# A quarter of the first batch's up layer as seven block products, with the set-up of the weights reordered around it

## The chip, the cores and the metric

One core of one Trainium2 chip. The time is the device time of one execution in microseconds; the numbers compared are medians over runs, and the traces are one profiled execution each. Engines: TensorE (PE in the profile, its weight loads PEld), VectorE (DVE), ScalarE (ACT), GpSimd (POOL), SyncE (SP).

## The reference

Linear attention with projected keys and values, and then a feed-forward layer with a maximum of two linear maps:

```
k_proj = E @ k,  v_proj = F @ v                       # per batch and head: 64 x 64
attn   = softmax(q @ k_proj.T / 8) @ v_proj
x      = attn, heads side by side                     # 8192 tokens x 512
out    = maximum(x @ w1, x @ w2) @ w_out              # w1, w2: 512 x 1024, w_out: 1024 x 512
```

Batch 8, 8 heads, sequence 1024, head size 64. Inputs and output are float32; the kernel works in float16 with float32 sums.

## The kernel before

**What is computed.** maximum(a, b) = relu(a - b) + b, so with wd = w1 - w2 and m = w2 @ w_out the output is relu(x @ wd) @ w_out + x @ m. relu(x @ wd) is the "up" layer, the rest the "down" layer. Each batch is cut into two units of 512 tokens; U[b, o] is unit o of batch b.

**Seven products.** From unit U[1, 0] on the up layer, for all units the down layer, and once the product m = w2 @ w_out, go by seven block products in place of eight (Strassen's scheme in Winograd's form). The factors are cut into 2 x 2 blocks; VectorE makes four sums or differences of each factor: of x (sums_x into s_x), of the up layer's result g (sums_g into s_g), of w2 transposed (sums_m), of w_out and m (step_t into T_sb), of wd (step_tw into t_w). The products run in the order 1, 2, 6, 5, 7, 3, 4. Products 1, 6, 7 and 4 add up in one PSUM bank (X) which ScalarE copies out after 1, 6 and 7 (keep) because the running sums are needed; 2 has a bank (Y); 5 and 3 share that bank again (Z). The blocks of the result are additions of these on VectorE.

**Batch 0.** Its up layer is done directly, in pieces: up_slots(t, j) gives eight pieces u_j[0] to u_j[7] for unit j (u0 and u1), each of four matmuls of 128 x 512 (line 525) into one bank, emptied by a relu on ScalarE (line 534; for piece 3 on VectorE, line 536). Meanwhile the weights arrive and are prepared: step_wd and step_wd_rows (wd[1], wd[2], wd[3] are the second, third and fourth quarter of the columns of wd = w1 - w2, on VectorE, line 549), and step_w2t (w2 transposed by TensorE in four groups of eight 128 x 128 blocks, line 557, each copied out by ScalarE, line 563). The list `slots` gives the order in which all this is issued. m_steps, at its end, is the product m by seven products of eight matmuls of 256 columns (line 634).

**What sets the order.** The schedule is written by hand: the program order of `slots`, with further steps hung behind a slot by at_slot, is the order of every engine's queue; each engine takes its queue strictly in order, and semaphores make it wait for data and for buffers. After batch 0's pieces come the slots ("P", n, p, i), the down products of unit n in pieces (line 838), with the attention of the next batches and their up products (up_steps, line 746) laid between them.

**Buffers.** PSUM has four banks mm0 to mm3 and two double banks "att". mm_bank() without a number takes the four in turn, mm_bank(n=...) a given one. In SBUF `box` names the large buffers big0 to big3 that held E and F, w1, w2 and the transposed w2 and are used again for the sums once those are read. `soft` has five tiles for exponentials and sums of the attention; `ppool` holds the copies that keep makes.

Of the kernel before, what the change touches and what calls it, by code (L numbers as in the profile page):

```python
# [9 lines left out]
FP32 = mybir.dt.float32  # L10
# [9 lines left out]
def kernel(  # L20
# [495 lines left out]
    def up_slots(t, j):  # L516
        t["gt", j] = gt = gpool.tile([128, NFB, HALF], FP16, tag="gt", name="gt_sb")
        for fb in range(NFB):
            def up(fb=fb, r0=0, r1=NDC):
                if r0 == 0:  # L520
                    t["up", j, fb] = mm_bank(n=None if r1 == NDC else first_banks[j][fb])
                h_ps = t["up", j, fb]
                order = range(NDC) if fb < 2 else (0, 2, 1, 3)
                for r in order[r0:r1]:
                    nc.tensor.matmul(  # L525
                        out=h_ps,
                        lhsT=wd_sb[:, r, fb * 128 : (fb + 1) * 128],
                        rhs=t["xt"][:, r, :, j * W : (j + 1) * W],
                        start=(r == 0), stop=(r == NDC - 1),
                    )  # L530
                if r1 < NDC:
                    return
                if fb != 3:
                    nc.scalar.activation(out=gt[:, fb, :], in_=h_ps, func=ACTF.Relu)
                else:
                    nc.vector.tensor_scalar_max(gt[:, fb, :], h_ps, 0.0)
            yield up
# [78 lines left out]
    def m_steps():  # L616
        st = {}
        two = lambda ap: ap.rearrange("q (i m) -> q i m", i=2)

        def product(k, name, n):  # L620
            if n is not None:
                st[name] = mm_bank(n=n)
            bank = st[name]
            Bb = lambda h, c: wo_sb[:, h * NG : (h + 1) * NG, c * CH : (c + 1) * CH]
            T = lambda i: T_sb[:, i, 0:NG, :]
            a, w_ = {
                1: lambda: (m_blk(0, 0), Bb(0, 0)), 2: lambda: (m_blk(0, 1), Bb(1, 0)),
                3: lambda: (m_sums[3], Bb(1, 1)), 4: lambda: (m_blk(1, 1), T(3)),
                5: lambda: (m_sums[0], T(0)), 6: lambda: (m_sums[1], T(1)),
                7: lambda: (m_sums[2], T(2)),  # L630
            }[k]()
            for i in range(2):
                for c in range(NG):
                    nc.tensor.matmul(  # L634
                        out=bank[:, i * CH : (i + 1) * CH],
                        lhsT=a[:, c, i * 128 : (i + 1) * 128],
                        rhs=w_[:, c, :],
                        start=(n is not None and i == 0 and c == 0),
                        stop=(c == NG - 1), skip_group_check=True,
                    )  # L640
            return bank

        def block(j, c):
            return m_sb[:, 2 * j : 2 * j + 2, c * CH : (c + 1) * CH]

        def add(j, c, x, y):
            nc.vector.tensor_tensor(out=block(j, c), in0=two(x), in1=two(y), op=ALU.add)
# [23 lines left out]
        return [p1, p2, p6, p5, p7, p3, p4]  # L671

    def s_g(i):
        return box[2].rearrange("q (s n m) -> q s n m", s=4, n=NG)[:, i]

    def s_x(i, u):
        n = u["n"] % 3
        half = box[1 if n < 2 else 3].rearrange("q (h s n m) -> q h s n m", h=2, s=4, n=NX)
        return half[:, n % 2, i]

    def t_w(i):
        return box[0].rearrange("q (s n m) -> q s n m", s=4, n=NX)[:, i]

    def step_tw(i):
        sub4(
            [t_w(i) for i in range(4)],
            lambda h, c: wd_sb[:, h * NX : (h + 1) * NX, c * HALF : (c + 1) * HALF], (i,),
        )

    def x_blk(u, j, h):  # L690
# [25 lines left out]
        step_s(u, g_blk, s_g, which)  # L716

    def keep(tag, bank, copy=nc.scalar.copy):
        x = ppool.tile([128, 512], FP32, tag=tag, bufs={"pu": 3, "pd": 4}[tag], name="p_sb")
        copy(out=x, in_=bank)  # L720
        return x

    def new_gt(u):
        u["gt"] = gpool.tile([128, NFB, HALF], FP16, tag="gt", name="gt_sb")


    def up_steps(u):
        for d in range(2):
            st = {}
            xbank, ybank = (2, 3) if d == 0 else (3, 2)  # L730

            def product(k, name, n, st=st, d=d):
                if n is not None:
# [21 lines left out]
            two = lambda ap: ap.rearrange("q (m n) -> q m n", m=2)  # L755

            def c_blk(j, c, d=d):
                return u["gt"][:, c * NG + 2 * d : c * NG + 2 * d + 2, j * W : (j + 1) * W]
# [4 lines left out]
            def relu(ap):  # L763
                nc.vector.tensor_scalar_max(ap, ap, 0.0)  # L764

            def p1(st=st, product=product, xbank=xbank, d=d):
                if d == 0:
                    new_gt(u)
                st["s1"] = keep("pu", product(1, "X", xbank))

            def p2(st=st, product=product, ybank=ybank, add=add, c_blk=c_blk):
                add(0, 0, product(2, "Y", ybank), st["s1"])
                relu(c_blk(0, 0))

            def p6(st=st, product=product):
                st["u1"] = keep("pu", product(6, "X", None))

            def p5(st=st, product=product, ybank=ybank):
                st["s5"] = keep("pu", product(5, "Z", ybank))

            def p7(st=st, product=product):
                st["u2"] = keep("pu", product(7, "X", None))
# [230 lines left out]
    def loads(b, *names):  # L1013
        for n in names:
# [12 lines left out]
            elif b_ < B:  # L1027
                load_all(tiles[b_], b_, n, {"k": k, "v": v, "q": q}[n])

    slots = [  # L1030
        (0, lambda: u0[0](r0=2)), (1, lambda: u0[1](r0=2)), (None, lambda: loads(1, "v", "q", "k")),
        (None, lambda: step_w2t(256, True)),
        (2, lambda: u1[0](r0=2)), (3, lambda: u1[1](r0=2)),
        (None, wd[1]), (4, u0[2]), (5, u0[3]),
        (None, wd[2]), (6, u1[2]), (7, u1[3]), (None, wt[2]), (None, wt[3]), (8, u0[4]), (9, u0[5]), (None, wd[3]),
        (10, u1[4]), (11, u1[5]), (12, u0[6]), (13, u0[7]),
        (14, u1[6]), (15, u1[7]),
        *((16 + n, x) for n, x in enumerate(m_steps())),
    ]
    slots = [((0, n), x) for n, x in slots]  # L1040

# [27 lines left out]
        steps.setdefault(key, []).append(lambda: s(*a))  # L1069


    for key, s_, *a in (
        *((10 + i // 2, sums_m, i) for i in range(4)), *((12 + i, step_t, 0, (i,)) for i in range(4)),
        (11, open_box, 1), (11, sums_x, U[0, 0], (0, 1)),
        (15, open_box, 0, 2), (17, sums_x, U[0, 0], (2, 3)),
        (18, sums_g, U[0, 0], (0, 1)), (19, sums_g, U[0, 0], (2, 3)), (22, open_box, 3),
    ):
        at_slot((0, key), s_, *a)


    t = tiles[1]
    at_slot((0, 22), new_attn, t)
    at_slot((0, 22), lambda: turn.__setitem__(slice(None), [2, 3]))
    for n, x in enumerate((
        "", "", "", "", "", "kv", "", "kpt", "qt00 qt10", "", "sc00 sc10", "qt01",
        "qt11 dn00 in00 dn10 in10", "", "", "at00 AT10 sc01",
    )):
        key = ("P", n // 15, (n - 1) // 2 % 7, (n - 1) % 2) if n else (0, 22)
        for name in x.split():
            if name[0] == "k":  # L1090
                if name == "kpt":
# [12 lines left out]
        if n in (2, 3):  # L1104
            for i in range(2):
                at_slot(key, step_tw, 2 * (n - 2) + i)
        if 6 <= n < 10:
            at_slot(key, sums_x, U[0, 1], ((2, 0, 1, 3)[n - 6],))


    t = tiles[2]
# [252 lines left out]
```

## Time and profile before

| | |
|---|---|
| median of 3 runs | 319.89 us (319.88 to 319.95) |
| the profiled execution, its own time | 320.29 us |
| its span, first to last instruction | 318.5 us |
| granted TensorE clock, mean | 1.000 |
| TensorE busy | 311.8 us (98%) |
| VectorE, ScalarE, GpSimd busy | 241.1, 206.0, 41.4 us |
| matmuls of the direct up pieces (line 525) | 64, from 23.8 us on |
| first matmul of m (line 634), first of the down products (line 838) | 39.4 us, 45.5 us |

Timeline rows show the start, the length, the engine, the line, the operation with its tiles, the shapes and the count of instructions merged into one row; an idle time of the engine just ahead of it stands in brackets with what ended it. A matmul's row ends when its last result is out, so rows of TensorE overlap and its pace is read from starts.

### The profile page before, as it was taken

The numbers are of one execution on the slowest core, as the hardware profiler recorded it, in microseconds if no ns is written. First come the engines' busy times: TensorE is split into PE (matmuls) and PEld (weight loads), VectorE is DVE, ScalarE is ACT, GpSimd is POOL, SyncE is SP. The second block draws the span as 40 slices with busy tenths as digits, with TensorE's granted clock in tenths as the row PEclk, the third lists the DMA queues.
The fourth block names the chain that finished last, engine by engine and source line by source line (L and its number), as shares of the span: only waits on it lengthen the run. The fifth ranks groups of instructions, "written<-read, shape, count | busy, mean of one in ns | idle before, by whom it ended". The sixth has DMA issues, their size and how long they took to land.

```text
span 318.5 us, 9309 instructions
## 1 busy us (share of the span) xinstructions
PE 311.8 (98%) x3922; PEld 253.8 (80%) x3922; DVE 241.1 (76%) x442; ACT 206.0 (65%) x373; POOL 41.4 (13%) x63
## 2 busy tenths in 40 slices
PE   7999999999999999999999999999999999999996
PEld 3565588888887888788887888788887888888885
DVE  2366889887969696896969696996969696969883
ACT  2386742777776777477776777477776777765541
POOL 8259102004000300012000400030000000000000
PEclk9999999999999999999999999999999999999999
DMA  7999999999989999799999999989979131313124
GB/s 179 206 202 197 207 207 201 207 156 141 204 163 183 171 209 245 208 188 147 225 229 219 169 199 245 221 155 174 230 153 217 42 101 36 102 35 102 36 99 136
DMA packets 76684, 53.71 MB, mean 169 GB/s; under 512 B 29664, under 2 KB 76128, under 8 KB 76640
## 3 DMA queue, kind: packets, MB, share of 16 engines
q0 software_dynamic: 30688, 28.05, 56.0%
q1 hardware_dynamic: 45664, 24.85, 33.1%
q8 instruction: 31, 0.51, 0.6%
q10 hardware_dynamic: 288, 0.20, 0.2%
q14 instruction: 13, 0.11, 0.1%
HBM read 57.15 MB, written 16.78 MB: 232 GB/s over the span
## 4 chain that ended last, share of the span: by engine, by line
PE 95%; DMA 3%; ACT 1%; DVE 1%; issue 0%; POOLq 0%
PE mm_ps L838 47%; PE mm_ps L746 27%; PE mm_ps L525 4%; PE mm_ps L195 4%; PE att_ps L352 4%; PE mm_ps L340 2%; DMA k_sb<-in_k_dram 2%; PE mm_ps L634 2%; PE att_ps L237 1%; PE mm_ps L311 1%; PE mm_ps L153 1%; DMA out_dram<-o_sb 1%; PE att_ps L340 0%; DVE qt_sb L316 0%; ACT ld_sb L388 0%
## 5 line engine op out<-in xcount | busy, mean ns | idle before, releaser
L720 ACT COPY p_sb<-mm_ps 128x512 f32<-128x512 f32 x179 | 101.7, 592 | 49.2 <-PE mm_ps L746 27.3
L838 PEld LDWEIGHTS <-big 128*128 128x128 f16 x768 | 73.5, 98 | 11.8 <-issue 3.6
L838 PE MATMUL mm_ps<-T_sb,big 128*128 128x256 f16 x576 | 76.9, 273 | 0.0
L761 DVE TENSOR_TENSOR gt_sb<-mm_ps,p_sb 128x512 f16<-128x512 f32 x56 | 38.5, 688 | 43.0 <-PE mm_ps L746 41.6
L746 PE MATMUL mm_ps<-big,big 128*128 128x256 f16 x336 | 50.4, 273 | 0.0
L746 PEld LDWEIGHTS <-big 128*128 128x128 f16 x448 | 43.8, 98 | 5.1
L838 PE MATMUL mm_ps<-wo_sb,gt_sb 128*128 128x256 f16 x256 | 42.6, 273 | 0.0
L838 PEld LDWEIGHTS <-gt_sb 128*128 128x128 f16 x376 | 35.7, 98 | 6.7 <-issue 2.7
L469 ACT ACTIVATE ex_sb<-mm_ps 128x512 f16<-128x512 f32 x50 | 27.2, 597 | 18.0 <-PE mm_ps L340 12.3
L746 PEld LDWEIGHTS <-wd_sb 128*128 128x128 f16 x336 | 32.9, 98 | 3.8
L746 PE MATMUL mm_ps<-xt_sb,wd_sb 128*128 128x256 f16 x224 | 32.8, 273 | 0.0
L499 DVE TENSOR_TENSOR xt_sb<-att_ps,ld_sb 128x1024 f16<-128x1024 f32 x26 | 31.7, 1219 | 0.2
L303 POOL COPY junk<-qt_sb 1x1 f16<-1x1 f16 x6 | 2.6, 432 | 172.3 <-DMA qt_sb<-q_sb 172.3
L838 PE MATMUL mm_ps<-m_sb,xt_sb 128*128 128x256 f16 x128 | 24.4, 273 | 0.0
L869 DVE TENSOR_TENSOR o_sb<-mm_ps,p_sb 128x512 f32<-128x512 f32 x32 | 21.9, 683 | 2.8 <-ACT p_sb L898 2.0
L764 DVE TENSOR_SCALAR gt_sb<-gt_sb 128x512 f16<-128x512 f16 (+1 forms) x60 | 20.9, 348 | 2.1
L706 DVE TENSOR_TENSOR big<-gt_sb 128x1024 f16<-128x1024 f16 x32 | 21.9, 683 | 0.0
L838 PE MATMUL mm_ps<-wo_sb,big 128*128 128x256 f16 x128 | 21.5, 273 | 0.0
L807 ACT ACTIVATE gt_sb<-mm_ps 128x512 f16<-128x512 f32 x28 | 16.8, 601 | 5.7 <-PE mm_ps L746 5.7
L838 PE MATMUL mm_ps<-T_sb,gt_sb 128*128 128x256 f16 x120 | 20.3, 273 | 0.0
L838 PEld LDWEIGHTS <-xt_sb 128*128 128x128 f16 x188 | 18.3, 98 | 2.3 <-issue 0.2
L761 DVE TENSOR_TENSOR gt_sb<-p_sb 128x512 f16<-128x512 f32 x28 | 19.1, 682 | 0.6 <-ACT p_sb L720 0.6
(121 smaller groups left out, 434.8 us busy)
## 6 DMA issues: line engine op xcount, KB each, us to landing
out_dram<-o_sb SPq DMA_DIRECT2D x62, 256.0 KB
k_sb<-in_k_dram POOLq DMA_DIRECT2D x7, 1024.0 KB, 9.7
v_sb<-in_v_dram POOLq DMA_DIRECT2D x7, 1024.0 KB, 15.4
q_sb<-in_q_dram POOLq DMA_DIRECT2D x5, 1024.0 KB, 22.8
q_sb<-in_q_dram POOLq DMA_DIRECT2D x6, 512.0 KB, 15.9
big<-in_moe_w_dram POOLq DMA_DIRECT2D x12, 128.0 KB, 6.4
v_sb<-in_v_dram POOLq DMA_DIRECT2D x4, 256.0 KB, 14.0
wo_sb<-in_moe_w_out_dram POOLq DMA_DIRECT2D x1, 1024.0 KB, 10.4
```

Source lines behind the costliest of these rows:

```text
L195: nc.tensor.matmul(out=kv_ps[r * KP : (r + 1) * KP, h * D : (h + nh) * D], lhsT=eft[i][:, c, :], rhs=t[w][:, h0 + h : h0 + h + nh, c, :], ...
L352: nc.tensor.matmul(out=dst(r ^ (hh % 2))[hh * Z : (hh + 1) * Z, :], lhsT=weights(rows, hh), rhs=ex[rows, hh % 2, hh // 2 * W : (hh // 2 + ...
L469: nc.scalar.activation(out=t["ex", g, j][:, e, :], in_=banks[e], func=ACTF.Exp, scale=scale)
L499: nc.vector.tensor_tensor(out=x_out(t, g, j).rearrange("q z o n -> q o z n"), in0=at_ps.rearrange("q o (z n) -> q o z n", z=2), in1=ld[:, ...
L706: nc.vector.tensor_tensor(out=S(i), in0=S(0) if x is None else x, in1=y(), op=op)
L720: copy(out=x, in_=bank)
L746: nc.tensor.matmul(out=bank[:, m * W : (m + 1) * W], lhsT=w_[:, n_, (2 * d + m) * 128 : (2 * d + m + 1) * 128], rhs=a[:, n_, :], start=(n ...
L761: nc.vector.tensor_tensor(out=c_blk(j, c), in0=two(x), in1=two(y), op=ALU.add)
L764: nc.vector.tensor_scalar_max(ap, ap, 0.0)
L807: nc.scalar.activation(out=out, in_=in_, func=ACTF.Relu)
L838: nc.tensor.matmul(out=bank[i][:, 0:CH] if two_banks else bank[:, i * CH : (i + 1) * CH], lhsT=a(c)[:, i * 128 : (i + 1) * 128], rhs=w_(c) ...
L869: nc.vector.tensor_tensor(out=o_sb, in0=two(x), in1=two(y), op=ALU.add)
```

## The change

- Four of the sixteen pieces of batch 0's up layer, u1[2], u1[3], u1[6] and u1[7], that is half of the columns' pairs of unit U[0, 1], are computed by seven block products, up_steps(U[0, 1], (1,)), called S1, S2, S6, S5, S7, S3, S4 below. They use banks 2 and 3, and keep their copies in `soft` tiles.
- The remaining direct pieces after the first four use bank fb % 2 (0 or 1), where they took the four banks in turn.
- The last two transposed groups of w2 go to the attention banks. The first chain of m's products (M1, M6, M7, M4) also uses an attention bank, M2 bank 0 and M5 and M3 bank 1, so m's products use three tiles.
- The first addition of the quarter (c0, after S2) is put behind the third weight difference, and its last two additions with their relu (rest) go into the down products. The first addition of m's product (M_add) goes behind two sums of g.
- The differences of wd, t_w, are made in two halves of their columns: step_tw(i, 1) ahead of S6, step_tw(i, 0) in the down products, where the x sums of U[0, 1] were; those now come first, ahead of u0[2].
- The x sums of units with n % 3 below 2 and the g sums go to the parts of w1's and w2's buffers that are read out, without opening these buffers anew.
- What was hung behind slots by at_slot in this section is written into `slots` itself.

```diff
-                    t["up", j, fb] = mm_bank(n=None if r1 == NDC else first_banks[j][fb])
+                    t["up", j, fb] = mm_bank(n=first_banks[j][fb] if r1 < NDC else fb % 2)
...
-                st[name] = mm_bank(n=n)
+                st[name] = att_banks()[:, 0, :] if n == 3 else mm_bank(n=n)
...
-            st["s1"] = keep("pu", product(1, "X", 2))
+            st["s1"] = keep("pu", product(1, "X", 3))
...
-            add(0, 0, product(2, "Y", 3), st["s1"])
+            st["c0"] = product(2, "Y", 0)
...
-    def step_tw(i):
+    def step_tw(i, d):
+        f0 = d * CH
         sub4(
-            [t_w(i) for i in range(4)],
-            lambda h, c: wd_sb[:, h * NX : (h + 1) * NX, c * HALF : (c + 1) * HALF], (i,),
+            [t_w(i)[:, :, f0 : f0 + CH] for i in range(4)],
+            lambda h, c: wd_sb[:, h * NX : (h + 1) * NX, c * HALF + f0 : c * HALF + f0 + CH], (i,),
         )
...
-    def up_steps(u):
-        for d in range(2):
+    def up_steps(u, halves=range(2)):
+        for d in halves:
             st = {}
-            xbank, ybank = (2, 3) if d == 0 else (3, 2)
+            tag = "soft" if u["b"] == 0 else "pu"
+            xbank, ybank = (2, 3) if d == 0 or u["b"] == 0 else (3, 2)
...
+                bank = product(2, "Y", ybank)
+
+                def c0():
+                    add(0, 0, bank, st["s1"])
+                    relu(c_blk(0, 0))
+
+                if u["b"] == 0:
+                    u["c0"] = c0
+                else:
+                    c0()
...
+                if u["b"] == 0:
+                    def rest(u=u, st=st, d=d, bank=bank):
+                        add(0, 1, bank, st["u1"])
+                        add(1, 1, st["u2"], st["s5"])
+                        relu(up_gt(u)[:, NG + 2 * d : NG + 2 * d + 2, :])
+
+                    u["rest"] = rest
+                    return
...
-        (0, lambda: u0[0](r0=2)), (1, lambda: u0[1](r0=2)), (None, lambda: loads(1, "v", "q", "k")),
-        (None, lambda: step_w2t(256, True)),
-        (2, lambda: u1[0](r0=2)), (3, lambda: u1[1](r0=2)),
-        (None, wd[1]), (4, u0[2]), (5, u0[3]),
-        (None, wd[2]), (6, u1[2]), (7, u1[3]), (None, wt[2]), (None, wt[3]), (8, u0[4]), (9, u0[5]), (None, wd[3]),
-        (10, u1[4]), (11, u1[5]), (12, u0[6]), (13, u0[7]),
-        (14, u1[6]), (15, u1[7]),
-        *((16 + n, x) for n, x in enumerate(m_steps())),
+        lambda: u0[0](r0=2), lambda: u0[1](r0=2), lambda: loads(1, "v", "q", "k"),
+        lambda: step_w2t(256, True),
+        lambda: u1[0](r0=2), lambda: u1[1](r0=2), wd[1], lambda: sums_x(U[0, 1], range(4)),
+        u0[2], u0[3], S1, S2, lambda: step_w2t(512, True), lambda: step_w2t(768, True), wd[2],
+        lambda: U[0, 1]["c0"](), u0[4], u0[5], wd[3], lambda: [step_tw(i, 1) for i in range(4)] and None,
+        u1[4], S6, u1[5], S5, u0[6], S7, u0[7],
+        lambda: [sums_m(i) for i in range(4)] and None, S3, S4,
+        lambda: step_t(0, (0, 1)), M1, lambda: step_t(0, (2, 3)), M2, lambda: sums_x(U[0, 0], (0, 1)),
+        M6, lambda: sums_g(U[0, 0], (0, 1)), M_add, M5, lambda: sums_g(U[0, 0], (2, 3)), M7, M3, M4,
...
+        if n == 2:
+            at_slot(key, sums_x, U[0, 0], (2, 3))
+        if n == 3:
+            at_slot(key, lambda: U[0, 1]["rest"]())
         if 6 <= n < 10:
-            at_slot(key, sums_x, U[0, 1], ((2, 0, 1, 3)[n - 6],))
+            at_slot(key, step_tw, n - 6, 0)
```

More of the change, by code (lines that the diff above doesn't have):

```diff
@@ L1028, in loads @@
                 load_all(tiles[b_], b_, n, {"k": k, "v": v, "q": q}[n])
+    open_box(0)
+    S1, S2, S6, S5, S7, S3, S4 = up_steps(U[0, 1], (1,))
+    M1, M2, M6, M5, M7, M3, M4, M_add = m_steps()
     slots = [
-        (0, lambda: u0[0](r0=2)), (1, lambda: u0[1](r0=2)), (None, lambda: loads(1, "v", "q", "k")),
-        (None, lambda: step_w2t(256, True)),
-        (2, lambda: u1[0](r0=2)), (3, lambda: u1[1](r0=2)),
-        (None, wd[1]), (4, u0[2]), (5, u0[3]),
-        (None, wd[2]), (6, u1[2]), (7, u1[3]), (None, wt[2]), (None, wt[3]), (8, u0[4]), (9, u0[5]), (None, wd[3]),
-        (10, u1[4]), (11, u1[5]), (12, u0[6]), (13, u0[7]),
-        (14, u1[6]), (15, u1[7]),
-        *((16 + n, x) for n, x in enumerate(m_steps())),
+        lambda: u0[0](r0=2), lambda: u0[1](r0=2), lambda: loads(1, "v", "q", "k"),
[7 more added lines that the diff above has]
+        M6, lambda: sums_g(U[0, 0], (0, 1)), M_add, M5, lambda: sums_g(U[0, 0], (2, 3)), M7, M3, M4,
+        lambda: (open_box(3), new_attn(tiles[1]), turn.__setitem__(slice(None), [2, 3])) and None,
     ]
-    slots = [((0, n), x) for n, x in slots]
+    slots = [(("M", n), x) for n, x in enumerate(slots)]
     kv_units = range(3, 2 * B - 4, 2)
@@ L1069, in at_slot @@
         steps.setdefault(key, []).append(lambda: s(*a))
[L1072 to L1078, printed above, removed]
     t = tiles[1]
-    at_slot((0, 22), new_attn, t)
-    at_slot((0, 22), lambda: turn.__setitem__(slice(None), [2, 3]))
     for n, x in enumerate((
```

42 lines of the change are left out of this document (22 added, 20 removed).

## The prediction

> **What bounds the kernel now.** I read the page first (busy shares, then the chain that ended last), then TensorE's own waits, then the timeline of each engine from 27 to 60 us, where the change lies.
>
> ```profile
> span 318.5 us, 9309 instructions
> PE 311.8 (98%) x3922; PEld 253.8 (80%) x3922; DVE 241.1 (76%) x442; ACT 206.0 (65%) x373; POOL 41.4 (13%) x63
> PE 95%; DMA 3%; ACT 1%; DVE 1%; issue 0%; POOLq 0%
> PE att_ps L352 <- ACT vp_sb L207: 0.5, 1, 0.5
> PE att_ps L352 <- ACT ex_sb L380: 0.3, 1, 0.3
> PE att_ps L340 <- DVE qt_sb L316: 0.2, 1, 0.2
> ```
>
> The first three lines say that TensorE is busy for 98% of the span and is 95% of the chain. The last three, from TensorE's list of waits (us in all, times, longest), are the only ones after the first microseconds in which it waits for another compute engine. So a microsecond that TensorE saves in the middle is a microsecond of the span, and a wait put into the middle costs its whole length: nothing later is idle that could absorb it. The 0.2% that a measurement can tell is 0.64 us here.
>
> ```profile
> 27.31 4.48 PE L525 MATMUL mm_ps<-xt_sb,wd_sb 128*128 128x512 f16 x20
> 31.63 1.06 PE L557 MATMUL mm_ps<-ident,big 128*128 128x128 f16 x16
> 32.52 7.07 PE L525 MATMUL mm_ps<-xt_sb,wd_sb 128*128 128x512 f16 x32
> 39.43 1.91 PE L634 MATMUL mm_ps<-wo_sb,big 128*128 128x256 f16 x16
> 41.17 2.78 PE L634 MATMUL mm_ps<-T_sb,p_sb 128*128 128x256 f16 x24
> 43.80 1.04 PE L634 MATMUL mm_ps<-wo_sb,p_sb 128*128 128x256 f16 x8
> 44.67 1.04 PE L634 MATMUL mm_ps<-T_sb,big 128*128 128x256 f16 x8
> 45.54 0.60 PE L838 MATMUL mm_ps<-wo_sb,gt_sb 128*128 128x256 f16 x4
> ```
>
> These are timeline rows: start, length, engine and line, and the releaser of an idle time in brackets. None has a bracket, so the stretch is gapless, and the starts give the pitches: 32 matmuls of 512 columns in 39.43 - 32.52 = 6.91 us, 0.216 each; 56 of 256 columns in 45.54 - 39.43 = 6.11 us, 0.109 each; 16 transposes in 32.52 - 31.63 = 0.89 us. The last column sums leave the array later than the pitch: a timeline row's length is its count times the pitch plus 0.16 (7.07 against 6.91).
>
> **1. TensorE's own work: -0.40 us.** The instruction order of the changed kernel shows four pieces u1[2], u1[3], u1[6], u1[7] gone, 16 matmuls of 512 columns (16 x 0.216 = 3.46 us), and seven products S1 to S7 of four 256-column matmuls each instead (28 x 0.109 = 3.06 us). The transposes of w2, the 56 matmuls of w2 @ w_out and everything later keep count and shape.
>
> **2. Where the new order puts TensorE.** From 27.31: u1[0] and u1[1] (their second halves), u0[2], u0[3] are 12 x 0.216, to 29.90; S1 to 30.34, S2 to 30.77; the two transpose groups to 31.22 and 31.66, their last results out 0.16 later (31.38 for the first); u0[4] to 32.53, its result out at 32.69; u0[5] to 33.39; then u1[4]. The transposes and u0[4] come 0.86 us earlier than before (30.77 and 31.66 against 31.63 and 32.52), since S1 and S2 stand in front of them where u1[2] and u1[3] stood, in half their time.
>
> **3. The wait that I forecast: +0.49 us.** Before, mm_bank() without a number turned through four banks. Now u0[4], u0[5], u1[4], u1[5], u0[6], u0[7] use bank fb % 2, so u1[4] needs the bank of u0[4], with u0[5] alone between them. It is ScalarE that empties it, after the two copies of the transposed w2.
>
> ```profile
> 28.97 1.62 ACT L534 ACTIVATE gt_sb<-mm_ps 128x512 f16<-128x512 f32 x3
> 32.27 1.93 ACT L563 COPY big<-mm_ps 128x1024 f16<-128x1024 f16 x2 [0.71 <-PE mm_ps L557]
> 34.09 1.82 ACT L534 ACTIVATE gt_sb<-mm_ps 128x512 f16<-128x512 f32 x3
> 36.17 0.60 ACT L534 ACTIVATE gt_sb<-mm_ps 128x512 f16<-128x512 f32 x1 [0.27 <-PE mm_ps L525]
> 20.85 1.02 ACT L380 ACTIVATE ex_sb<-att_ps 128x1024 f16<-128x1024 f32 x1
> 21.92 0.30 PE L352 MATMUL att_ps<-ex_sb,ones 64*32 64x256 f16 x8 [0.28 <-ACT ex_sb L380]
> ```
>
> Already before, u0[4]'s relu started late: its result was out at 32.52 + 4 x 0.216 + 0.16 = 33.54, the relu began at 34.09, when the copies let ScalarE go, 1.82 us after the first copy began (34.09 - 32.27). Four banks hid that. Now: ScalarE is free of the three relus (28.97 + 1.62 = 30.59) and does S1's copy at about 30.53 to 31.1; the first transposed group is out at 31.38, its copy starts 0.03 later at 31.41; u0[4]'s relu starts at 31.41 + 1.82 = 33.23 and takes 0.60: 33.83. TensorE restarts about 0.05 after ScalarE's end (21.92 against 20.85 + 1.02 = 21.87, the last two rows): 33.88. It wanted to start at 33.39. The wait is 0.49 us. No work of TensorE stands behind u1[4] that could go ahead: S6, u1[5] and the rest are queued behind it.
>
> The Trainium skill, page "ScalarE: Activation LUTs", section "What ACT_TABLE_LOAD costs", gives 186 ns + 0.833 ns per element for an instruction and 93 ns of overlap between neighbours; by an estimate from that, two copies hold ScalarE 1.89 us instead of the 1.82 of the row, the wait would be 0.56 and the sum +0.16. The trace does not quite agree, and the sum goes by its row.
>
> **4. What is late next: the differences on VectorE.** S6 needs t_w(1), the second of four half-size differences that now run behind c0 (the first block sum of S1 and S2, with its relu) and the last weight difference.
>
> ```profile
> 30.10 0.69 DVE L536 TENSOR_SCALAR gt_sb<-mm_ps 128x512 f16<-128x512 f32 x1 [2.46 <-PE mm_ps L525]
> 30.71 0.84 DVE L549 TENSOR_TENSOR wd_sb<-big,big 128x512 f16<-128x512 f16 x2
> 32.44 0.75 DVE L549 TENSOR_TENSOR wd_sb<-big,big 128x512 f16<-128x512 f16 x2
> 34.23 0.69 DVE L706 TENSOR_TENSOR p_sb<-big 128x1024 f16<-128x1024 f16 x1 [1.05 <-ACT big L563]
> 37.57 0.68 DVE L597 TENSOR_TENSOR T_sb<-wo_sb 128x1024 f16<-128x1024 f16 x1
> 41.45 0.69 DVE L647 TENSOR_TENSOR m_sb<-mm_ps,p_sb 128x512 f16<-128x512 f32 x1 [1.26 <-PE mm_ps L634]
> 46.46 0.42 DVE L597 TENSOR_TENSOR T_sb<-m_sb 128x512 f16<-128x512 f16 x1
> 46.91 0.42 DVE L597 TENSOR_TENSOR T_sb<-m_sb,T_sb 128x512 f16<-128x512 f16 x1
> 47.25 0.68 DVE L597 TENSOR_TENSOR big<-wd_sb 128x1024 f16<-128x1024 f16 x1
> L764 DVE TENSOR_SCALAR gt_sb<-gt_sb 128x512 f16<-128x512 f16 x36 | 10.6, 294 | 1.2
> ```
>
> u0[3]'s relu stays at 30.10 (its result is out at 27.31 + 12 x 0.216 + 0.16 = 30.06), the third weight difference runs 30.71 to 31.55, just ahead of u0[4] at 31.66. Should it be up to 0.5 us later, nothing is lost: u0[4]'s result (32.69) lies until 33.23 before ScalarE takes it. c0's addition, like L647's, takes 0.69 from about 31.5 (S1's copy is done at 31.1, S2 is out at 30.93), its relu 0.29 (L764), to 32.5; the fourth weight difference 0.75 to 0.84, to 33.3; a half-size difference has the shape of the L597 rows at 46.46, 0.45 to the next one that depends on it and 0.34 to one that does not, so t_w(1) is done at 33.3 + 0.45 + 0.42 = 34.17. S6 wants to start at 33.88 + 4 x 0.216 = 34.74: 0.57 to spare, at no cost. If the wait of part 3 were gone, S6 would come at 34.25, with only 0.08 to spare.
>
> **5. The rest of the section, at nothing, with its cover.** The rows for it, of VectorE, TensorE, GpSimd's transfers, the transfers' times to landing (last number) and one stretch with its granted clock (third number from the end):
>
> ```profile
> 36.78 0.42 DVE L706 TENSOR_TENSOR big<-xt_sb 128x512 f16<-128x512 f16 x1
> 49.78 0.69 DVE L869 TENSOR_TENSOR o_sb<-mm_ps,p_sb 128x512 f32<-128x512 f32 x1
> 53.87 1.47 PE L838 MATMUL mm_ps<-T_sb,big 128*128 128x256 f16 x12
> 21.98 5.05 POOL L139 DMA_DIRECT2D big<-in_moe_w_dram x7 [0.63 <-DMA v_sb<-in_v_dram]
> 27.03 0.88 POOL L143 DMA_DIRECT2D wo_sb<-in_moe_w_out_dram  x1
> big<-in_moe_w_dram POOLq DMA_DIRECT2D x12, 128.0 KB, 6.4
> wo_sb<-in_moe_w_out_dram POOLq DMA_DIRECT2D x1, 1024.0 KB, 10.4
> 21.90:23.30 1.40, 0.92 (x32) 0.63 (x36) 1.40 (x3) 1.40 (x4) 1.32 (x2) 1.00 1.44 196
> ```
>
> S6, S5, S7 and S4 give ScalarE four more passes of about 0.6, less three relus. From u1[4] on TensorE spends 4 x 0.216 + 4 x 0.109 = 1.30 us on each pair of them, ScalarE two of its pitches, (1.62 - 0.60) / 2 = 0.51 each, so it keeps up; the closest is S7's copy, done at 38.6, ahead of S4 at 39.08. VectorE is done with the half-size differences at 34.85; the four sums of w2 take 2.5 us as before (34.23 to 36.78) and the four differences of w_out 2.5 more, to 40.0. M6, the first product to read either, starts at 39.52 + 16 x 0.109 = 41.26 (39.52: 33.88, then u1[4], u1[5], u0[6], u0[7] and S6, S5, S7, S3, S4, 16 x 0.216 + 20 x 0.109). M1's copy stands to M6 as before. M_add is through by 42.8 and its bank 0 is next used at 45.63, where the first down product starts: cover 2.8 us. M1's bank among the attention banks was emptied by the copy of the first transposed group at 32.4.
>
> w_out lands at 27.03 + 10.4 = 37.43, so its differences cannot start at 37.3; that 0.1 is in the 40.0. In the down products four full differences of wd (47.25 to 49.78, 2.5 us) make way for two x sums (0.34 each) and the rest of the quarter (two additions of 0.6 and a relu of 0.43), 2.3 us; the four x sums after them make way for four half-size differences of the same shape. Nobody on TensorE reads the moved ones before 53.87 (P7's differences of m) or later, so I cost this at nothing; if VectorE fell behind by more than the about 1 us between the output addition at 49.78 and the reuse of its bank by P5 at 51.4, each further microsecond would count in full. The queues of SP and of GpSimd have the same transfers in the same order.
>
> **The sum.** -0.40 + 0.49 = +0.09 us. The profiled execution, 320.29 us with a span of 318.5, would become 320.38; it lies 0.40 above the median of the runs, 319.89, so on the median's scale the changed kernel takes 319.98, rounded to **320.0 us**. What the wait can be: nothing (-0.40 in all), or, with each of ScalarE's four steps 0.05 later, 0.7 (+0.3).
>
> **The rivals.** *No wait for ScalarE* (19%): the copies of the attention banks are released earlier, or the piece waits less than worked out, and only the 0.40 less of matmuls is left, with up to 0.08 lost before S6: 319.5 to 319.6. For it: nothing on TensorE waited here before. Against: the relu at 34.09, 0.55 after its input was there, shows the backlog already.
>
> *The differences come last* (15%), the one on the slower side: S6 waits on VectorE for t_w(1), whose source is the last piece of w1. That transfer is issued at about 21.98 + 6 x 0.72 = 26.3 and at the median of 6.4 lands at 32.7; the fourth weight difference wants its second half at 32.9. It decides once it lands after 33.4, and costs over 0.64 us in all once it lands after 34.0; landing at 34.4 gives S6 at 35.7 and 321.0 us. For it: the w transfers are bunched with k, v and q at this point, and c0 sits in front of the difference. Against: before, the same difference ran at 32.44 with no wait for a transfer.
>
> *TensorE's clock drops in the new wait* (2%): run at half the granted clock, every microsecond of the section costs another one, 0.55 us of it would make the kernel slower by 0.2%, and the 5.6 us from 33.88 to 39.5 would give 325.6. The Trainium skill, page "TensorE: Matmul & The Clock Gate", section "A second HAM failure mode: psum-queue depth-cycling", says that small idle times between groups that cycle through PSUM banks can make the clock swing between half and full; that is a rule against this change. The row at 21.90 speaks against it here: 0.48 us idle in 1.40 us, at a granted clock of 1.00.
>
> **How the numbers follow.** The forecast has 58%, and its own range is 319.8 to 320.3. With the first rival's 19% the range reaches down to 319.45; with the nearer part of the second up to 320.8, beyond which I leave 11% of it. Of the rest, 6%, I give 4 to a gain that no row shows (faster by over 0.2% needs 0.64 us, and the matmuls give 0.40) and 2 to VectorE's backlog in the down products. Faster: 4%. Within 0.2%: 58 + 19 = 77%. Slower: 15 + 2 + 2 = 19%.
>
> **What would show it right or wrong.** In the profile after: no column-512 matmul rows for the four pieces and 28 new rows of 256 columns in up_steps at 0.109; the transposes at about 30.8; ScalarE's relu of u0[4] at 33.2; an idle time of TensorE of 0.4 to 0.6 before u1[4], released by ScalarE, the only new entry in its list of waits; S6 following u1[4] without a wait; the first down product at about 45.6. I am wrong in part 3 if that idle time is absent or TensorE waits elsewhere, and in part 5 if the first down product starts near 45.6 and the span still moves by over 0.3 us.

## The result and the profile after

The changed kernel takes 321.09 us (median of 6 runs, 320.85 to 321.18) against 319.88 us of the kernel before (6 runs beside it): a ratio of 1.0038, 95% interval 1.0026 to 1.0051, that is 0.83 to 1.63 us slower. The profiled execution takes 320.99 us. From the page of the changed kernel (span, busy shares, the chain that ended last), and two entries of TensorE's list of waits:

```profile
span 319.2 us, 9349 instructions
PE 312.3 (98%) x3934; PEld 255.0 (80%) x3934; DVE 243.8 (76%) x450; ACT 206.8 (65%) x375; POOL 40.2 (13%) x63
PE 91%; DMA 5%; ACT 2%; POOL 1%; issue 0%; DVE 0%; POOLq 0%
```

```profile
PE mm_ps L1217 <- DMA out_dram<-o_sb: 1.5, 1, 1.5
PE mm_ps L525 <- ACT gt_sb L534: 0.3, 1, 0.3
```

TensorE is as busy as before. The last line is the wait that was forecast. The one above it is the small matmul at the very end, which waits for the last stores.

TensorE's timeline of the changed section, then ScalarE's and VectorE's rows that set its waits:

```profile
27.06 2.75 PE L525 MATMUL mm_ps<-xt_sb,wd_sb 128*128 128x512 f16 x12
29.65 1.04 PE L756 MATMUL mm_ps<-xt_sb,wd_sb 128*128 128x256 f16 x8
30.52 1.06 PE L557 MATMUL att_ps<-ident,big 128*128 128x128 f16 x16
31.42 1.89 PE L525 MATMUL mm_ps<-xt_sb,wd_sb 128*128 128x512 f16 x8
33.65 1.02 PE L525 MATMUL mm_ps<-xt_sb,wd_sb 128*128 128x512 f16 x4 [0.34 <-ACT gt_sb L534]
34.59 0.61 PE L756 MATMUL mm_ps<-big,big 128*128 128x256 f16 x4
39.37 1.04 PE L634 MATMUL att_ps<-wo_sb,big 128*128 128x256 f16 x8
45.48 0.60 PE L864 MATMUL mm_ps<-wo_sb,gt_sb 128*128 128x256 f16 x4
31.17 1.93 ACT L563 COPY big<-att_ps 128x1024 f16<-128x1024 f16 x2 [0.30 <-PE att_ps L557]
32.98 1.11 ACT L534 ACTIVATE gt_sb<-mm_ps 128x512 f16<-128x512 f32 x2
31.18 0.42 DVE L549 TENSOR_TENSOR wd_sb<-big,big 128x512 f16<-128x512 f16 x1 [0.30 <-DMA big<-in_moe_w_dram]
32.24 0.71 DVE L774 TENSOR_SCALAR gt_sb<-gt_sb 128x512 f16<-128x512 f16 x1
34.10 0.42 DVE L597 TENSOR_TENSOR big<-wd_sb,big 128x512 f16<-128x512 f16 x1
```

I call the time from u1[0]'s second half to the first down product the stretch: 45.48 - 27.06 = 18.42 us, before 45.54 - 27.31 = 18.23. So it is 0.19 longer, and that is not the 1.2 us. u1[4] was wanted at 31.42 + 8 x 0.216 = 33.15 and started at 33.65: 0.50 (the 0.34 in its bracket counts from the end of the row before, which lies 0.16 after the pitch). S6 was wanted at 33.65 + 4 x 0.216 = 34.51 and started at 34.59, behind t_w(1) (34.10 + 0.42): 0.08.

The rest lies at the other end. The last pair of matmuls of the down products and VectorE's additions into the last output tile, of the kernel before and then of the changed one:

```profile
315.15 0.28 PE L931 MATMUL mm_ps<-T_sb,xt_sb 128*128 128x128 f16 x2
314.85 0.91 DVE L937 TENSOR_TENSOR o_sb<-mm_ps,p_sb 128x256 f32<-128x256 f32 x3 [0.29 <-PE mm_ps L931]
```

```profile
315.10 0.28 PE L957 MATMUL mm_ps<-T_sb,xt_sb 128*128 128x128 f16 x2
315.16 0.82 DVE L963 TENSOR_TENSOR o_sb<-mm_ps,p_sb 128x256 f32<-128x256 f32 x3 [0.66 <-PE mm_ps L957]
```

From the first down product to this last pair the two kernels agree to 0.01 us: 315.15 - 45.54 = 269.61 and 315.10 - 45.48 = 269.62. But the tail, which I count from the start of the very last matmul of the pair (0.05 after its row) to the end of the span, is 3.31 us before and 4.06 after: +0.75. VectorE's first addition starts 0.36 before that last matmul in the one and 0.01 behind it in the other; its idle time in brackets is 0.66 instead of 0.29, though TensorE and ScalarE had its inputs ready at the same distance in both traces.

The transfer view of one microsecond of the tail (315.6 to 316.6: queue, packets, MB, share of the 16 transfer engines), of before and then of the changed kernel, shows the other half:

```profile
q1 hardware_dynamic: 169, 0.15, 45.7%
q10 hardware_dynamic: 161, 0.14, 43.1%
```

```profile
q1 hardware_dynamic: 181, 0.17, 51.5%
q10 hardware_dynamic: 98, 0.08, 25.5%
q14 instruction: 1, 0.01, 3.1%
```

In the changed kernel there is an 8 KB fetch of instructions among the last stores (the third line); the kernel before has none in this microsecond. Of the last store's 16 landings 15 come by 2.64 us after the last matmul's start (before: all 16 by 2.29), and one at 3.04. So the 0.75 is made of 0.35, by which the 15 are later, about as much as VectorE's start, and of 0.40 for the one landing that is late. The sum of stretch and tail is 0.19 + 0.75 = 0.94 us. The profiled executions differ by 0.70, because the stretch happened to begin 0.25 earlier after (27.06 against 27.31). The medians differ by 1.21, whose interval holds the 0.94; the 0.27 between them I can't place, since the stretch's start alone lies between 26.63 and 27.31 us in the eight profiles in which the start was not edited on TensorE.

### The profile page after: what moved, and what is told of

The parts are those of the page before. It is cut to its first block, busy times and chain, and to the rows that moved or that the text cites. A ratio compares the mean times of both kernels' runs of the same rounds, so it can differ in the third digit from the quotient of the medians.

```text
span 319.2 us, 9349 instructions
## 1 busy us (share of the span) xinstructions
PE 312.3 (98%) x3934; PEld 255.0 (80%) x3934; DVE 243.8 (76%) x450; ACT 206.8 (65%) x375; POOL 40.2 (13%) x63
## 4 chain that ended last, share of the span: by engine, by line
PE 91%; DMA 5%; ACT 2%; POOL 1%; issue 0%; DVE 0%; POOLq 0%
PE mm_ps L864 47%; PE mm_ps L756 28%; DMA v_sb<-in_v_dram 4%; PE att_ps L352 3%; PE mm_ps L195 3%; PE mm_ps L525 3%; PE mm_ps L340 2%; PE att_ps L237 1%; PE att_ps L634 1%; PE mm_ps L634 1%; DMA out_dram<-o_sb 1%; ACT big L563 1%; PE mm_ps L311 1%; POOL k_sb L108 0%; POOL q_sb L108 0%; PE att_ps L557 0%
## 5 line engine op out<-in xcount | busy, mean ns | idle before, releaser
L864 PEld LDWEIGHTS <-big 128*128 128x128 f16 x768 | 73.5, 98 | 11.8 <-issue 3.6
L771 DVE TENSOR_TENSOR gt_sb<-mm_ps,p_sb 128x512 f16<-128x512 f32 x58 | 39.8, 686 | 42.8 <-PE mm_ps L756 41.2
L756 PE MATMUL mm_ps<-big,big 128*128 128x256 f16 x348 | 52.2, 273 | 0.0
L756 PEld LDWEIGHTS <-big 128*128 128x128 f16 x464 | 45.3, 98 | 6.1 <-DVE big L597 0.4
L864 PEld LDWEIGHTS <-gt_sb 128*128 128x128 f16 x376 | 35.7, 98 | 6.7 <-issue 2.7
L756 PEld LDWEIGHTS <-wd_sb 128*128 128x128 f16 x348 | 34.0, 98 | 4.4
L756 PE MATMUL mm_ps<-xt_sb,wd_sb 128*128 128x256 f16 x232 | 33.8, 272 | 0.0
L774 DVE TENSOR_SCALAR gt_sb<-gt_sb 128x512 f16<-128x512 f16 (+1 forms) x62 | 22.4, 362 | 2.1
L303 POOL COPY junk<-qt_sb 1x1 f16<-1x1 f16 x6 | 1.7, 290 | 172.8 <-DMA qt_sb<-q_sb 172.8
```

Source lines behind the costliest of these rows:

```text
L756: nc.tensor.matmul(out=bank[:, m * W : (m + 1) * W], lhsT=w_[:, n_, (2 * d + m) * 128 : (2 * d + m + 1) * 128], rhs=a[:, n_, :], start=(n ...
L864: nc.tensor.matmul(out=bank[i][:, 0:CH] if two_banks else bank[:, i * CH : (i + 1) * CH], lhsT=a(c)[:, i * 128 : (i + 1) * 128], rhs=w_(c) ...
```

## The experiments

All times are medians beside runs of the kernel before on the same chip (319.81 us for the first four, 319.94 and 319.92 for the others). Stretch, tail and SyncE's time for issuing the store 1.14 us before the last matmul are from one profile each; from the first down product to the last matmul's start it is 269.67 to 269.78 us in every kernel. The ratios are those on record with their intervals; they need not be the quotients of the medians.

| kernel | time us | ratio, interval | stretch | tail | SyncE's issue |
|---|---|---|---|---|---|
| before | 319.88 | | 18.23 | 3.31 | 0.42 |
| after | 321.09 | 1.0038 (1.0026 to 1.0051) | 18.42 | 4.06 | 1.30 |
| b_pad48 | 323.38 | 1.0100 (1.0063 to 1.0136) | 18.23 | 3.37 | 0.86 |
| b_pad78 | 322.68 | 1.0049 (1.0016 to 1.0082) | 18.23 | 3.31 | 0.42 |
| a_pad78 | 323.48 | 1.0098 (1.0063 to 1.0133) | 18.34 | 4.05 | 0.42 |
| a_fix78 | 322.40 | 1.0080 (1.0057 to 1.0102) | 17.83 | 4.06 | 0.42 |
| b_dve12 | 320.65 | 1.0022 (1.0013 to 1.0031) | 18.23 | 4.04 | 0.42 |
| a_dve16 | 320.45 | 1.0017 (1.0007 to 1.0026) | 18.41 | 3.46 | 1.05 |
| a_fix | 320.60 | 1.0017 (1.0003 to 1.0030) | 17.93 | 4.19 | 0.94 |
| a_fix_dve16 | 319.91 | 0.9996 (0.9987 to 1.0005) | 17.83 | 3.63 | 1.22 |
| a_att | 320.89 | 1.0024 (1.0004 to 1.0044) | 18.09 | 3.94 | 0.42 |
| a_c0 | 320.84 | 1.0020 (0.9997 to 1.0043) | 18.34 | 4.13 | 1.17 |
| a_fix_d16_p16 | 320.04 | 1.0001 (0.9981 to 1.0020) | 17.83 | 3.61 | 1.21 |
| a_fix_d16_p26 | 320.41 | 1.0007 (0.9989 to 1.0026) | 17.83 | 3.45 | 1.05 |

Stretch and tail are set against the medians of all runs, so one more thing has to be said. Their sum, counted from the kernel before, agrees with the difference of the medians to 0.08 us in b_dve12, a_fix, a_fix_dve16 and a_c0. It falls short by 0.18 in a_dve16, 0.22 in a_fix_d16_p16, 0.27 in the changed kernel, 0.48 in a_att and 0.75 in a_fix_d16_p26. In a_dve16, a_att and a_fix_d16_p26 the profiled execution itself lies 0.30, 0.43 and 0.55 us below the kernel's median, so part of the median is in no trace here; the rest stays open.

### TensorE's instruction fetch in the tail (b_pad48, b_pad78, a_pad78, a_fix78)

The first suspicion was TensorE's own instructions. The change adds 12 matmuls with their weight loads, 24 instructions, and the trace has a 16 KB instruction fetch 1.43 us before the last matmul, where the kernel before has none (its nearest is 13.18 us before). The trace does not name the engine of a fetch; I take the 16 KB ones as TensorE's, since the last of them ahead of the end come when it has begun 7331, 7587 and 7844 instructions, about 256 apart. Theory F puts the tail down to that fetch, Theory O to the changed order of the work. The fetch was moved by cutting warm-up matmuls at the start into four:

```diff
-            nc.tensor.matmul(out=w_ps, lhsT=ones16[:, 0:128], rhs=ones16, start=True, stop=True)
+            c = i % parts * m          # m = 512 // parts, n * parts of them
+            nc.tensor.matmul(out=w_ps[:, c : c + m], lhsT=ones16[:, 0:128], rhs=ones16[:, c : c + m], start=True, stop=True)
...
-    warm(8)
+    warm(8, 4)
-    warm(5)
+    warm(5, 4)                         # not in b_pad48
```

b_pad48 is the kernel before with 48 TensorE instructions more, b_pad78 with 78, a_pad78 the changed kernel with 78. a_fix78 is a_pad78 with the two edits of a_fix, below.

> The kernel before with its first eight warm-up matmuls of 512 columns cut into four of 128 columns each: the same TensorE time, 48 more TensorE instructions, nothing of the change. Theory F (fetch): TensorE's instructions come in blocks of 16 KB, about 256 instructions; in the kernel before the last block is not asked for until the end, and any 30 to 60 more instructions bring one block's transfer into the last 2 us, where it holds up one of the sixteen DMA engines under the last stores. Then this kernel has a block fetched at about 314 us, the last stores land about 0.7 us later behind the last matmul, and it takes 320.6 us although nothing else is changed. Theory O (order): the later end of the changed kernel comes from its own work, for instance from VectorE's order; then this kernel takes 319.9.

> The same for the first thirteen warm-up matmuls, 78 more TensorE instructions. Theory F: the block is asked for about 80 instructions ahead of the end, near 312 us, and is through before the last stores are issued: 319.9, as before. Theory O: 319.9 as well. It shows what the cut warm-up itself costs; a kernel slower by 0.3 or more here would make the cut the cause in the run above.

> The changed kernel with the same 78 more TensorE instructions in the warm-up. Theory F: the last block is fetched about 120 instructions ahead of the end, near 310 us, the last stores land as in the kernel before, 0.7 us earlier than in the changed kernel: 320.35. What then is left over the kernel before is the new waits in the section, 0.2, and the start. Theory O: 321.1, as the changed kernel.

> The changed kernel with the same 78 instructions, with u1[4] in an attention bank (so that it needs not wait for the relu of u0[4]) and with the first addition c0 behind the four half-size differences (so that S6 need not wait for the second of them). My working of the section: both waits, 0.50 and 0.08, go and the 0.40 less of matmuls is left: the section from the first instruction of u1[0]'s second half to the first down product takes 17.8 us instead of 18.4. Theory F: 319.5 to 319.8. Theory O: 320.5, since the end stays late. If S6 still waits, the last weight difference is late by its transfer, and 0.1 to 0.3 of it stays.

The times can't be used: with the warm-ups cut, TensorE idled in the start. TensorE's timeline rows of b_pad48, and below it of b_pad78, with one of its windows (third number from the end: granted clock):

```profile
24.93 0.29 PE L354 MATMUL att_ps<-ex_sb,vp_sb 64*32 64x256 f16 x5 [1.70 <-issue]
```

```profile
24.65 0.82 PE L354 MATMUL att_ps<-ex_sb,vp_sb 64*32 64x256 f16 x20 [1.08 <-issue]
```

```profile
25.00:27.00 2.00, 2.00 (x23) 0.59 (x5) 1.84 (x4) 0.00 (x0) 1.99 (x4) 0.50 1.31 205
```

"issue" means that TensorE waited for nothing that the profile shows. A 16 KB instruction fetch of TensorE begins shortly ahead of it (22.50 us in b_pad48, 22.20 in b_pad78), while the inputs fill the transfer engines; that it is late for that reason was not tried. The tails can be used, and Theory F, as the cause of the 0.75, fell by them: in b_pad48 the fetch is 1.66 us before the last matmul and the tail is 3.37, and in a_pad78 and a_fix78 it is out of the way (5.5 us before the last matmul) and the tail is still 4.05 and 4.06.

### VectorE's instruction count (b_dve12, a_dve16)

The same fetches exist for VectorE. Counting semaphore and control instructions too, its trace has 574 rows before and 586 after. In both kernels 8 KB fetches come when it has begun 67 or 68, 195 to 198, 318 to 325 and 447 or 448 rows, about 128 apart; the changed kernel has a fifth at 579, in the tail. I take these as VectorE's by that distance. There are other 8 KB fetches; four of them come at such counts of ScalarE's rows (65 or 66, 187 to 193, 320 to 324, 446 or 447).

The addition that starts late is VectorE's 576th row, that is 64 + 4 x 128. Theory V: it is the count, not the order of the work. The Trainium skill, page "Perfetto Trace Analysis", section "Per-instruction lifecycle: what the profiler-reported window actually captures", gives 64 bytes for an instruction; by an estimate from that, 8 KB hold 128, which agrees with the distances in these traces. Twelve and sixteen more VectorE instructions were made by cutting the cast at 2.7 us, behind which VectorE idles for over 3 us:

```diff
-    nc.vector.tensor_copy(out=ident16, in_=ident)
+    cut = [9 * i for i in range(13)] + [128]           # b_dve12; a_dve16: 7 * i, range(17)
+    for a, b in zip(cut, cut[1:]):
+        nc.vector.tensor_copy(out=ident16[:, a:b], in_=ident[:, a:b])
```

> The kernel before, with one VectorE instruction, the cast of the identity at about 2.7 us, cut in 13, where VectorE then idles for 3.4 us: 12 instructions more on VectorE, the number of rows that the change adds there (574 to 586), and nothing else. Theory V (the tail's 0.75 us comes from the count of VectorE's instructions: the addition that is its 576th row starts 0.37 us late, and an 8 KB fetch of instructions, 0.7 to 1.1 us after the last matmul, holds up one of the 16 transfer engines that carry the last stores by 0.40): the first addition into the last output tile starts 0.01 us after the last matmul's start instead of 0.36 before it, the tail (last matmul's start to the end of the span) is 4.05 us instead of 3.31, the time 319.88 + 0.75 = 320.6 us. Theory O (the tail is owed to the changed order of the work, or to the other engines): tail 3.31 us and 319.9 us. Both: the stretch from u1[0]'s second half to the first down product stays 18.23 us.

> The changed kernel, with the cast of the identity at about 2.7 us cut in 17: 16 instructions more on VectorE. Theory V: VectorE's 576th row is now what was its 560th, an addition or relu at about 305 us behind which VectorE idles; the fetch comes at about 306 us, ahead of the last stores; the tail is 3.31 us again and the time 321.09 - 0.75 = 320.35 us. Theory O: tail 4.05 us and 321.1 us. Both: the stretch to the first down product stays at 18.4 us.

VectorE's and TensorE's rows of the tail of b_dve12 and a line of its transfer view (315.6 to 316.6 us), then the rows of a_dve16:

```profile
314.92 0.82 DVE L939 TENSOR_TENSOR o_sb<-mm_ps,p_sb 128x256 f32<-128x256 f32 x3 [0.66 <-PE mm_ps L933]
314.85 0.28 PE L933 MATMUL mm_ps<-T_sb,xt_sb 128*128 128x128 f16 x2
```

```profile
q14 instruction: 1, 0.01, 1.9%
```

```profile
314.50 0.91 DVE L965 TENSOR_TENSOR o_sb<-mm_ps,p_sb 128x256 f32<-128x256 f32 x3 [0.29 <-PE mm_ps L959]
314.80 0.28 PE L959 MATMUL mm_ps<-T_sb,xt_sb 128*128 128x128 f16 x2
```

This settles that the count does it. The kernel before, with twelve tiny casts more at its start and nothing else changed, has the changed kernel's tail: the 0.66 us of idle time, the fetch (the third line), one landing at 3.02 us with the other 15 by 2.64, 4.04 us in all, and 320.65 us against 320.6 forecast by Theory V. The changed kernel with sixteen more loses the late start, and its fetch moves 11.3 us ahead of the last matmul; 320.45 against 320.35 forecast. Theory O fell in both. In a_dve16 the 576th row is an addition that waits 0.64 us for ScalarE in any case; nothing is lost there.

a_dve16's tail is 3.46 us, not 3.31. The column of SyncE's issue says what is left: where TensorE's fetch lies 1.4 to 1.7 us before the last matmul, that issue takes 0.86 to 1.30 us instead of 0.42, and with VectorE out of the way the tail follows it: 3.31 at 0.42, 3.37 at 0.86, 3.45 and 3.46 at 1.05, 3.61 and 3.63 at 1.21 and 1.22. So Theory F holds in small, as far as three times that move together can show it: 0.06 to 0.32 us. In the changed kernel VectorE's late start covers it (4.06 with that fetch, 4.05 without it in a_pad78); in a_c0 and a_fix, with 4.13 and 4.19, not quite.

### The two waits of the stretch (a_att, a_c0, a_fix, a_fix_dve16)

a_att gives u1[4] an attention bank, which is free by then; a_c0 puts the first block sum behind the differences; a_fix does both; a_fix_dve16 adds the sixteen VectorE instructions.

```diff
-                    t["up", j, fb] = mm_bank(n=first_banks[j][fb] if r1 < NDC else fb % 2)
+                    t["up", j, fb] = (att_banks()[:, 0, :] if (j, fb) == (1, 4)
+                                      else mm_bank(n=first_banks[j][fb] if r1 < NDC else fb % 2))
...
-        lambda: U[0, 1]["c0"](), u0[4], u0[5], wd[3], lambda: [step_tw(i, 1) for i in range(4)] and None,
+        u0[4], u0[5], wd[3], lambda: [step_tw(i, 1) for i in range(4)] and None, lambda: U[0, 1]["c0"](),
```

> The changed kernel, with u1[4] in one of the attention banks (so that it does not wait for ScalarE's relu of u0[4]) and the first block sum c0 behind the four half-size weight differences (so that S6 does not wait for them). VectorE's count of instructions stays. By part 1 of the prediction the stretch from u1[0]'s second half to the first down product takes 18.23 - 0.40 = 17.83 us instead of 18.42, so 321.09 - 0.59 = 320.5 us. Theories V and O both leave the tail at 4.05 us. If one of the two waits has a successor, the stretch stays over 18.1 us and the time over 320.8.

> Both edits together: u1[4] in an attention bank, c0 behind the differences, and 16 VectorE instructions more at the start. Theory V: the stretch 17.83 us and the tail 3.31 us, 321.09 - 0.59 - 0.75 = 319.75 us, 0.1 below the kernel before, whose start may differ by a few tenths. Theory O: 17.83 and 4.05 us, 320.5 us.

> The changed kernel with one edit: u1[4] in an attention bank. Of the stretch's two waits this takes the first, 0.50 us, alone. If the two lie one behind the other (the reading of the changed kernel's rows: S6 started 7.53 us after u1[0]'s second half because t_w(1) was done then, and would have waited for it without the first wait too): S6 still starts at 7.5, the wait before it grows from 0.08 to 0.58 us, the stretch stays at 18.4 and the time at 321.1 us. If the wait for ScalarE is the whole price of the stretch (the prediction's part 4 with 0.08 us to spare): 17.9 and 320.6 us. The tail stays at 4.05 us in both.

> The changed kernel with the other edit: c0 behind the four half-size differences. u1[4] still waits 0.5 us for ScalarE, S6 no longer waits for VectorE: the stretch is 18.42 - 0.08 = 18.34 us and the time 321.0 us, if the waits lie one behind the other; 17.9 us and 320.6 us if c0 were the cause of both. Tail 4.05 us.

TensorE's rows of a_fix_dve16:

```profile
26.95 2.75 PE L528 MATMUL mm_ps<-xt_sb,wd_sb 128*128 128x512 f16 x12
31.31 1.89 PE L528 MATMUL mm_ps<-xt_sb,wd_sb 128*128 128x512 f16 x8
33.03 1.03 PE L528 MATMUL att_ps<-xt_sb,wd_sb 128*128 128x512 f16 x4
33.90 0.60 PE L759 MATMUL mm_ps<-big,big 128*128 128x256 f16 x4
44.78 0.60 PE L867 MATMUL mm_ps<-wo_sb,gt_sb 128*128 128x256 f16 x4
```

No gap is left: 44.78 - 26.95 = 17.83 us, exactly 0.40 below the 18.23 of before. That is the whole gain of the seven products. It is used up by a tail that is 0.32 longer: 319.91 us, the time of the kernel before within the interval. a_fix, with VectorE's count as it was, has a tail of 4.19 and 320.60 us. Its stretch is 17.93, not the 17.83 expected: S6 started 0.04 late behind t_w(1), whose weight difference had waited 0.85 us for its transfer, and the rest of the 0.09 I have not traced.

a_att and a_c0 take the stretch's waits apart. TensorE's rows of u1[4] and S6 with VectorE's t_w(1), of a_att, and u1[4] of a_c0:

```profile
33.06 1.03 PE L526 MATMUL att_ps<-xt_sb,wd_sb 128*128 128x512 f16 x4
34.18 0.61 PE L757 MATMUL mm_ps<-big,big 128*128 128x256 f16 x4
33.69 0.42 DVE L598 TENSOR_TENSOR big<-wd_sb,big 128x512 f16<-128x512 f16 x1
```

```profile
33.22 1.02 PE L525 MATMUL mm_ps<-xt_sb,wd_sb 128*128 128x512 f16 x4 [0.34 <-ACT gt_sb L534]
```

Without the first wait, S6 is wanted at 33.06 + 4 x 0.216 = 33.92 and waits until 34.18 for t_w(1): half of what the first edit saves is lost again, and the stretch is 18.09. Neither of the two expectations had that. By an estimate it would have been 18.4 if the third weight difference had waited for its transfer as in the changed kernel (18.09 and the 0.30 in the bracket of the row at 31.18), and in a_att's profile it did not. With c0 out of the way alone, u1[4] waits 0.50 as before and the stretch is 18.34, as expected of two waits one behind the other.

### TensorE's fetch a little earlier (a_fix_d16_p16, a_fix_d16_p26)

a_fix_dve16, with the first 8, or all 13, warm-up matmuls cut in two (warm(8, 2), warm(5, 2)).

> The kernel with both waits and VectorE's boundary removed (319.91 us, tail 3.63 us) and the first 8 warm-up matmuls of TensorE cut in two each: 16 TensorE instructions more, so that TensorE's 16 KB instruction fetch, 1.4 us before the last matmul's start, comes 16 x 0.055 = 0.9 us earlier. Theory F in its small form (what is left over the 3.31 us, 0.15 to 0.32, is that fetch, beside which SyncE's issue of a store took 1.05 to 1.22 us instead of 0.42): tail 3.3 to 3.4 us and 319.6 us. Without it: tail 3.6 and 319.9. Cut by 48 instructions the warm-ups starved TensorE in the start; if 16 do so too, the start shows it and the time is over 320.5 us.

> The same with all 13 warm-up matmuls cut in two: 26 instructions more, the fetch 1.4 us earlier, 2.8 us before the last matmul's start. Theory F in its small form: tail 3.31 us and 319.6 us; without it 3.6 and 319.9. With TensorE starved in the start: over 320.5 us.

Both missed. The fetch came 0.16 and 0.33 us earlier, not 0.9 and 1.4: it lies 1.56 and 1.73 us before the last matmul and still beside SyncE's issue (1.21 and 1.05 us). The tails, 3.61 and 3.45, go with that issue as above, but the fetch was not got out of the way, and the times show no gain; in a_fix_d16_p26, 320.41 us with a stretch and a tail that sum to 0.26 less than before, they do not even follow the profile. What places this fetch stays open, and so does a version that keeps the whole 0.40.

## Why the prediction was wrong, step by step

- **Part 1, -0.40 us: right.** a_fix_dve16, a_fix78 and the two last kernels have a stretch of 17.83 us, 0.40 less than before.
- **Part 2: right** to 0.01 us. From the start of the stretch S1 is at 2.59 us in both, the transposes at 3.46, u0[4] at 4.36 (4.35 forecast).
- **Part 3, the wait of 0.49 us: right.** It is 0.50. The copies began at 31.17 and the relu at 32.98, 4.11 and 5.92 us into the stretch; 4.10 and 5.92 were forecast. The estimate weighed there, from the Trainium skill, page "ScalarE: Activation LUTs", section "What ACT_TABLE_LOAD costs", was 1.89 us for the two copies. They took 32.98 - 31.17 = 1.81, close to the 1.82 of the kernel before's row, by which the sum went.
- **Part 4, t_w(1) at 6.86 us into the stretch: too early by 0.60** (34.52 - 27.06 = 7.46). The third weight difference waited 0.30 for the transfer of its second half, and c0's relu took 0.71 instead of 0.29. Of the 0.57 to spare nothing was left, and S6 waited 0.08. The rival "the differences come last" was this mechanism at a smaller size; behind a cured first wait it cost 0.26 us (a_att). That the rival's far case was priced at 321.0 us, close to the measured time, is chance: S6 was late by 0.08, not by the 35.7 - 34.74 = 0.96 that this price rests on.
- **Part 5 and the sum: the step that failed.** The sign that the prediction named for it came: the first down product starts at 45.48 us, where 45.6 was forecast, and yet the span moves by 0.7. VectorE did not fall behind, the 269.6 us of the down products are unchanged. But the sum was made on the stretch alone and took all else as it was, at nothing; the tail was not looked at. The change brings VectorE from 574 to 586 rows, so that there is now a 576th, with the fetch that goes with it, and it is the first addition into the last output tile. That term was missing: +0.75 us, against the +0.09 of the sum. With the 0.10 by which the stretch missed, the prediction's 319.98 becomes 320.83, just above the 320.8 to which its range reached with the rivals. The measured 321.09 is 0.26 more, the rest that could not be placed above.
- **The other rivals.** "No wait for ScalarE" is out by the row at 33.65. TensorE's clock stayed full around the wait, as the row below, of the windows of the changed kernel, shows (third number from the end: granted clock). The swing of the clock that the Trainium skill, page "TensorE: Matmul & The Clock Gate", section "A second HAM failure mode: psum-queue depth-cycling", tells of where small idle times are frequent did not follow this single wait; whether many such waits in a row would bring it, no run here shows.

```profile
33.20:33.70 0.50, 0.15 (x2) 0.05 (x1) 0.47 (x3) 0.50 (x2) 0.00 (x0) 1.00 1.24 207
```

## What to carry to other kernels

An edit in the middle of a kernel also changes how many instructions each engine has executed by the time of its last store, and what comes at fixed counts moves with it: compare the tails of two traces before explaining a difference by the edited section. A control that adds the same number of trivial instructions to the kernel before, where that engine is idle, tells the count from the work in one run. And price the second-latest arrival with the trace's worst rows for that operation, not with its usual ones, before counting on what stands to spare.

## What the runs showed of the hardware

- VectorE's 576th row started 0.37 us late in all seven kernels in which it was the addition that has to follow TensorE at once (the changed kernel and b_dve12 among them), and an 8 KB fetch came 0.7 to 1.3 us after the last matmul's start; in five of the seven one of the 16 landings of the last store was then 0.38 to 0.40 us behind the other 15, in a_fix 0.53, and in a_att 0.07, where the issue of that store took 0.68 us instead of 0.38 to 0.60. That the fetch makes that landing late was not tried apart from the count. At the 192nd, 320th and 448th rows, where VectorE had a backlog, no such gap shows. The Trainium skill, page "Perfetto Trace Analysis", section "DVE / Act Engine Instruction (TENSOR_ADD, Activation, etc)", has the sequencer push instructions into a queue and go on to the next. With a backlog in that queue a late sequencer would stay hidden, which agrees with these rows but is not shown by them. What VectorE's sequencer does in the 0.37 us no row shows.
- A 16 KB instruction fetch of TensorE beside a store's issue went with 0.86 to 1.30 us for that issue instead of 0.42, in all eight kernels that have one there.
- In the start, where the inputs fill the transfer engines, TensorE idled 0.6 to 1.7 us without a releaser once the warm-ups were cut and its instruction fetch had moved; in two of the four kernels (b_pad78 and a_pad78) the granted clock was then 0.50 from 25 to 27 us.
- The relu of c0, on VectorE, took 0.71 us at 32.24, while GpSimd issued the transfer of k (31.94 to 32.84), and 0.29 us in a_c0 at 34.86, when GpSimd issued nothing. Whether the one makes the other was not tried.
